# One decode step of attention and a gated MLP on one core: loading w_q in two pieces, partitions 0 to 31 and then 32 to 127

## The chip, the core and the metric

The kernel runs on one core of one Trainium2 chip. The metric is the device time of one execution in microseconds (us), lower is better. An execution is one launch of the whole program; the times before the change come from three of them.

## The reference

The reference is one token through a pre-normalised transformer block, with D = 640, 32 heads of 128, a key and a value cache of 4096 positions for each head, and an MLP of width 1728. All inputs are bf16. Cut to what matters:

```python
h  = x + attention(layernorm(x))
h2 = h + mlp(layernorm(h))

# attention: B = Sq = 1, Hq = Hkv = 32, Sk = 4096, Dh = 128
q = (x @ wq)                                  # 640 -> 32 heads x 128
scores = einsum("bhqd,bhkd->bhqk", q, k_cache) * Dh ** -0.5
o = einsum("bhqk,bhkd->bhqd", softmax(scores), v_cache)
out = o.reshape(B, Sq, Hq * Dh) @ wo          # 4096 -> 640

# mlp
mlp(y) = (gelu(y @ w_gate) * (y @ w_up)) @ w_down    # 640 -> 1728 -> 640
```

The two caches are 32 x 4096 x 128 elements each, 33.6 MB in bf16, and each of their elements is used once. w_q and w_o are 5.2 MB each, the three MLP matrices 2.2 MB each.

## The kernel before

Every byte is loaded once, and nearly all loads are issued by SP, in one fixed order written out in the program. A small class, `Sched`, records the instructions of each engine with the semaphore values that they wait for; at the end each engine's list is emitted in the order in which it was recorded.

The heads are worked on in four groups of eight (`HG`, `NG`). For a group g, the partition dimension holds head and position together: each of the 128 partitions has 256 positions of one head, so that a K or a V load is [128, 256 x 128], 64 KB a partition and 8.4 MB in all (`load_k` L250, `load_v` L254). Three large buffers, `big[0]` to `big[2]`, hold these tiles in turn. w_q also lies in `big[2]`, as five rows of the matrix to a partition: partition p has rows 5p to 5p + 4, 40 KB that are contiguous in memory (`wq_sb`). The matrices of the last stages lie in `big[2]` and `big[0]` when these have come free.

The order of SP's queue is: w_q (L257), K0, V0, K1, V1, K2, K3, V2, V3, w_o (L445), w_gate and w_up (L449), the tail of w_down (L456), w_down in four pieces (L461), and the output (L543). w_q, K0 and V0 wait for nothing. K1 goes to the buffer that holds w_q, and is issued when the query product has read all of it. Each later load waits for the last reader of its buffer, and since SP issues in order, what stands behind a waiting load waits too. ACT issues one small load, of x (L263).

The work on the compute engines is this:

- The norm of x gives `xb`, the normalised vector repeated over 128 columns (L280).
- `query(0)` and `query(2)` form q for two groups each: for each of the five rows that a partition holds, TensorE multiplies `xb[:, c, :]` with 512 columns of `wq_sb[:, c, :]` (first matmul of a row at L316, the others through `again`, L302). Each matmul contracts over all 128 partitions. `pick_q` on VectorE keeps, for each partition, the head that the partition belongs to (L324, L328), and ACT writes it to `qb` (L331).
- `scores(g)`: VectorE multiplies the K tile by q in four steps of 64 positions (L338), TensorE folds the 128 products of a position down to 16 (L352 and L302), VectorE sums the rest (L359).
- `soft(g)` and `values(g)`: the exponentials (L388), their spreading over head columns (L391), and the products with V on TensorE (L404). `outs(g)` gathers the output of the group (L412, L415).
- At the end come the product with w_o (L485), the second norm, the gate and up products (L503), GELU written out with an exponential, and the product with w_down (L538), whose result VectorE copies (L542) for the output load.

The load of w_q is one instruction and has a semaphore of its own, `d_wq`:

```python
d_wq = S.dma("sync", "wq", lambda s: s.dma_start(
    wq_sb[:, :, :], A_wq[:, :].rearrange("(p c) n -> p c n", c=NC_D)))
load_k(0, None)
load_v(0, None)
```

`S.dma` raises the semaphore by 16 for each call and returns the value that stands for "all calls so far under this name have landed".

## Time and profile before

| | |
|---|---|
| median of 3 runs | 202.99 us (202.74 to 203.08) |
| the profiled execution | 202.85 us, of which the span from first to last instruction is 201.6 us |
| granted TensorE clock, mean | 0.817 |
| TensorE matmul busy | 113.3 us (56%) |
| VectorE busy | 119.9 us (59%) |
| ScalarE, GpSimd busy | 9.7 us, 3.5 us |
| read from HBM | 84.23 MB, 418 GB/s over the span |
| w_q: size, issue to landing | 5120 KB, 15.0 us |
| TensorE's wait for w_q at L316 | 12.0 us |
| VectorE's wait for K loads at L338 | 19.0 us over three waits |

The profile cuts the span into 40 slices and gives the busy share of each engine in tenths; the DMA row is the mean over the 16 DMA engines of the core. The chain of waits is followed back from the last instruction: at each step to what released it. Windows of any length can be asked for, with the DMA share and the rate in each. The time from issue to landing of a load includes the time that it stands behind others in the queue. Times of single instructions and loads come from the one profiled execution.

### The profile page before, as it was taken

What the parts mean: (1) busy time and instruction counts of PE and PEld (TensorE: products, weight loads), DVE (VectorE), ACT (ScalarE), POOL (GpSimd) and SP (SyncE); (2) the same over time, 40 slices, a digit from 0 to 9 for tenths busy, and PEclk for the clock granted to TensorE, in tenths of its full rate; (3) what the DMA queues carried; (4) which work ended last, traced back from release to release, by engine and by line L of the source; (5) the groups of instructions that cost most, each with busy time, mean ns of one, the idle gap of its engine ahead of it and who ended that gap; (6) DMA issues with size and microseconds to landing.
All of it is one profiled execution on the core that took longest, in us unless ns stands there. A gap on an engine that the chain in (4) does not pass through costs nothing.

```text
span 201.6 us, 1614 instructions
## 1 busy us (share of the span) xinstructions
PE 113.3 (56%) x850; PEld 25.2 (13%) x560; DVE 119.9 (59%) x90; ACT 9.7 (5%) x27; POOL 3.5 (2%) x21
## 2 busy tenths in 40 slices
PE   1008910197508369876375059866634993945483
PEld 1000100000000032020031000200000032425431
DVE  1100650999993479997530499999899845000241
ACT  3000000000010101000101000000100011010000
POOL 5000000000000000000000000000000001000000
PEclk9999985579955858999958559999995799696558
DMA  7999999999999999999999999999999999999992
GB/s 260 406 569 416 429 416 416 416 416 416 416 429 533 455 442 406 429 416 416 429 418 419 416 429 533 442 416 429 429 416 416 429 416 444 406 390 432 411 414 90
DMA packets 2544, 84.32 MB, mean 418 GB/s; under 512 B 297, under 2 KB 490, under 8 KB 1002
## 3 DMA queue, kind: packets, MB, share of 16 engines
q1 hardware_dynamic: 2536, 84.23, 97.2%
q8 instruction: 5, 0.08, 0.2%
q10 hardware_dynamic: 2, 0.00, 0.0%
q14 instruction: 1, 0.01, 0.0%
HBM read 84.23 MB, written 0.00 MB: 418 GB/s over the span
## 4 chain that ended last, share of the span: by engine, by line
DMA 49%; DVE 33%; PE 13%; issue 2%; SPq 1%; ACT 1%
DMA big<-in_A_k_cache_dram 34%; DVE big L338 22%; DMA wd_sb<-in_B_w_down_dram 14%; PE pf L302 7%; DVE sc L359 5%; PE pv L404 5%; DVE P L391 2%; DVE xz L328 2%; DVE qm L324 1%; PE pf L352 1%; ACT ex L388 1%; SPq L461 1%; DVE mx L381 0%; SPq L449 0%; PE pf L538 0%
## 5 line engine op out<-in xcount | busy, mean ns | idle before, releaser
L338 DVE TENSOR_TENSOR big<-big,qb 128x8192 bf16<-128x8192 bf16 x16 | 70.2, 4418 | 19.0 <-DMA big<-in_A_k_cache_dram 19.0
L302 PE MATMUL pf<-big,Ibf 128*128 128x512 bf16 x240 | 61.6, 415 | 0.0
L352 PE MATMUL pf<-big,Ibf 128*128 128x512 bf16 x16 | 6.9, 433 | 48.0 <-DVE sc L359 24.4
L359 DVE TENSOR_REDUCE sc<-pf 128x64 f32<-128x1024 f32 x16 | 19.3, 1217 | 10.9 <-PE pf L302 10.9
L404 PE MATMUL pv<-big,P 128*32 128x512 bf16 x192 | 15.2, 487 | 2.8 <-DVE P L391 2.8
L352 PEld LDWEIGHTS pf<-big,Ibf 128*128 128x128 bf16 x16 | 1.6, 99 | 93.3 <-DVE sc L359 54.8
L324 DVE TENSOR_TENSOR qm<-pf,hmask 128x1024 f32<-128x1024 f32 x2 | 2.4, 1224 | 16.1 <-PE pf L302 16.1
L316 PE MATMUL pf<-wq_sb,xb 128*128 128x512 bf16 x5 | 2.4, 471 | 12.0 <-DMA wq_sb<-in_A_wq_dram 12.0
L391 DVE TENSOR_TENSOR P<-ex,hmask_bf 128x2048 bf16<-128x2048 bf16 x3 | 6.9, 2292 | 2.0 <-ACT ex L388 2.0
L328 DVE TENSOR_REDUCE xz<-qm 128x128 f32<-128x1024 f32 x4 | 7.5, 1880 | 0.1
L404 PEld LDWEIGHTS pv<-big,P 128*32 128x32 bf16 x192 | 5.9, 120 | 10.8 <-issue 5.3
L404 PE MATMUL pv<-big,Pl 128*32 128x512 bf16 x64 | 5.3, 507 | 2.8 <-DMA big<-in_A_v_cache_dram 2.8
L485 PE MATMUL pf<-wo_sb,aP 128*1 128x160 bf16 x128 | 4.4, 336 | 4.1 <-DMA wo_sb<-in_A_wo_dram 4.1
L388 ACT ACTIVATE ex<-sc,nb 128x256 bf16<-128x256 f32 x4 | 2.0, 508 | 85.8 <-DVE mj L385 85.8
L443 DVE TENSOR_TENSOR aT<-pm,rz 128x32 bf16<-128x32 f32 x1 | 0.2, 191 | 9.5 <-PE pm L415 9.5
L488 DVE STREAM_TRANSPOSE th<-pf 128x160 f32<-128x160 f32 x1 | 0.4, 351 | 9.0 <-PE pf L485 9.0
L399 PE MATMUL pm<-rsm,ones 128*128 128x8 f32 x8 | 1.8, 303 | 6.8 <-ACT rsm L395 6.8
L415 PEld LDWEIGHTS pm<-cred,xm 128*128 128x128 f32 x32 | 4.0, 191 | 8.9 <-issue 6.5
L302 PE MATMUL pf<-wq_sb,xb 128*128 128x512 bf16 x15 | 5.1, 458 | 0.0
L415 PE MATMUL pm<-cred,xm 128*128 128x8 f32 x32 | 4.0, 252 | 1.4 <-ACT xm L412 1.4
L485 PEld LDWEIGHTS pf<-wo_sb,aP 128*1 128x1 bf16 x128 | 4.1, 123 | 4.2 <-issue 4.2
L399 PEld LDWEIGHTS pm<-rsm,ones 128*128 128x128 f32 x8 | 1.7, 251 | 19.9 <-ACT rsm L395 16.5
(83 smaller groups left out, 53.2 us busy)
## 6 DMA issues: line engine op xcount, KB each, us to landing
wq_sb<-in_A_wq_dram SPq DMA_DIRECT2D x1, 5120.0 KB, 15.0
wo_sb<-in_A_wo_dram SPq DMA_DIRECT2D x1, 5120.0 KB, 20.4
wg_sb<-in_B_w_gate_dram SPq DMA_DIRECT2D x1, 2160.0 KB, 25.2
wu_sb<-in_B_w_up_dram SPq DMA_DIRECT2D x1, 1296.0 KB, 24.9
wu_sb<-in_B_w_up_dram SPq DMA_DIRECT2D x1, 864.0 KB, 26.6
wd_sb<-in_B_w_down_dram SPq DMA_DIRECT2D x1, 800.0 KB, 27.6
wd_sb<-in_B_w_down_dram SPq DMA_DIRECT2D x1, 640.0 KB, 28.5
wd_sb<-in_B_w_down_dram SPq DMA_DIRECT2D x1, 480.0 KB, 29.1
```

The costliest lines, as they stand in the source:

```text
L302: return t.add_instruction(m)
L324: a = t_qt[0] = vec(lambda v, i=i: v.tensor_tensor(out=qm[:, :, :], in0=pq[g][i][:, :].rearrange("p (h d) -> p h d", d=DH), in1=hmask[:, : ...
L328: t_qf[0] = vec(lambda v: v.reduce_sum(xz[:, :], qm[:, :, :].rearrange("p h d -> p d h"), axis=AX.X), [a, t_qb[gg - 1] if gg else None])
L338: return vec(lambda v: v.tensor_tensor(out=kb[g][:, s * RM:(s + 1) * RM, :], in0=kb[g][:, s * RM:(s + 1) * RM, :], in1=qb[:, g, :].unsquee ...
L352: return t.matmul(dst, Ibf[:, :], src, start=True, stop=False)
L359: red_done[n] = vec(lambda v: v.reduce_sum(sc[:, s * RM:(s + 1) * RM], pf[n % 2][:, :].rearrange("p (r w) -> p r w", r=RM), axis=AX.X), [f ...
L388: t_ex = S.op("scalar", lambda a: a.activation(ex[:, :], sc[:, :], ACTF.Exp, bias=nb[:, g:g + 1], scale=SCALE, accum_out=rs[:, g:g + 1]), ...
L391: t_p[g] = vec(lambda v: v.tensor_tensor(out=P[g][:, :, :], in0=ex[:, :].unsqueeze(2).to_broadcast([128, R, HG]), in1=hmask_bf[:, :].unsqu ...
L399: t_z[g] = S.op("tensor", lambda t: t.matmul(pz[:, 8 + g * HG:8 + (g + 1) * HG], ones[:, :], rsm[:, :], start=True, stop=True), [t_rs[g], ...
L404: t_pv[g] = S.op("tensor", lambda t, i=i, r=r, q=q: t.matmul(pv[g % 2][q:q + 32, :], P[g][:, r:r + VR, :], vb[g][:, r:r + VR, :], start=(i ...
L415: t_acc[g] = S.op("tensor", lambda t, r=r: t.matmul(po[:, g * HG:(g + 1) * HG], xm[:, r, :], cred[:, r * HG:(r + 1) * HG], start=(r == 0), ...
L485: b = S.op("tensor", lambda t, c=c, j=j: t.matmul(pd[32 * j:32 * j + 1, 0:NQ], aP[:, c:c + 1], wo_sb[:, c, j * NQ:(j + 1) * NQ], start=Fal ...
```

## The change

w_q is loaded by two instructions on SP instead of one: first the rows of partitions 0 to 31 (a quarter of the matrix), then those of partitions 32 to 127. Both raise the same semaphore, and the value that the query product waits for is now that of the second. The rows of a partition, their place in `wq_sb`, and everything behind the load are as before.

```diff
+QL = 32
...
-    d_wq = S.dma("sync", "wq", lambda s: s.dma_start(
-        wq_sb[:, :, :], A_wq[:, :].rearrange("(p c) n -> p c n", c=NC_D)))
+    for lo, hi in ((0, QL), (QL, 128)):
+        d_wq = S.dma("sync", "wq", lambda s, lo=lo, hi=hi: s.dma_start(
+            wq_sb[lo:hi, :, :], A_wq[:, :].rearrange("(p c) n -> p c n", c=NC_D)[lo:hi, :, :]))
     load_k(0, None)
     load_v(0, None)
```

## The prediction

> **What bounds the kernel now.** I read the slices of the page first, then the queues, the chain, the windows of the opening, and what the cache loads waited for.

> ```profile
> DMA  7999999999999999999999999999999999999992
> ...
> q1 hardware_dynamic: 2536, 84.23, 97.2%
> ...
> DMA 49%; DVE 33%; PE 13%; issue 2%; SPq 1%; ACT 1%
> ```

> The DMA engines are at nine tenths or more in every slice but the first and the last, and SP's queue alone fills 97.2% of their time. No compute engine passes 59% (VectorE, first part of the page). The chain of waits in order of time confirms it: whatever it follows, it comes back to transfers that take far longer than their own bytes.

> ```profile
> 1.25 33.87 DMA big<-in_A_k_cache_dram
> ...
> 78.45 35.15 DMA big<-in_A_k_cache_dram
> ...
> 169.73 29.15 DMA wd_sb<-in_B_w_down_dram
> ```

> The first K load is issued at 1.25 us, lands at 35.11, and the last w_down load lands at 198.88, some 2.7 us before the end. The windows of half a microsecond (the last two columns are the DMA share and GB/s) show how the loads are worked off. A packet is booked in the window in which it starts, so a share can pass 1.

> ```profile
> 4.00:4.50 0.50, 0.00 (x0) 0.00 (x0) 0.21 (x1) 0.26 (x1) 0.00 (x0) 1.00 2.65 1147
> 4.50:5.00 0.50, 0.00 (x0) 0.00 (x0) 0.23 (x1) 0.21 (x2) 0.00 (x0) 1.00 0.19 82
> 5.00:5.50 0.50, 0.00 (x0) 0.00 (x0) 0.50 (x1) 0.00 (x0) 0.00 (x0) 1.00 0.19 82
> 5.50:6.00 0.50, 0.00 (x0) 0.00 (x0) 0.22 (x1) 0.00 (x0) 0.00 (x0) 1.00 2.65 1147
> ...
> 14.50:15.00 0.50, 0.00 (x0) 0.00 (x0) 0.00 (x0) 0.00 (x0) 0.00 (x0) 1.00 4.25 1835
> ```

> There is a burst every 1.5 us. One period moves (1147 + 82 + 82) GB/s x 0.5 us = 655 KB, which is 16 rows of 40 KB: each of the 16 engines takes one partition's row of w_q per 1.5 us, so 27.3 GB/s per engine. The bursts start at about 1.5, 4.0, 5.5 and so on to 13.0: eight, because 128 rows over 16 engines are eight each. At 14.5 the rows become 64 KB: that is K, starting 1.5 us after the last w_q row, without a gap. K's bursts come 2.4 us apart (14.5, 17.0, 19.5), again 27.3 GB/s per engine. So the streams go in lockstep at one fixed pace, whichever tensor they read.

> ```profile
> DMA to landing us min/median/max: 26.5/35.4/52.8
> ```

> This is from the answer on the cache tiles. A cache load needs 8 x 2.4 = 19.2 us of its own, yet the quickest took 26.5 from issue to landing, so each found at least 7.3 us of work queued ahead of it. The rings never run dry between 1.5 and 197 us (mean share there 1.00). A delay of the opening is therefore carried to the end in full: nothing later has room to catch up, and later buffers come free by the same amount later.

> **The change part by part.** *One more issue on SP.* The w_q issue took 0.38 us and the next began 0.45 us after it (0.80 to 1.25). K's issue moves from 1.25 to about 1.70 and V's from 1.70 to about 2.15. Both hide behind the rows of w_q, which occupy the engines until 14.5: no cost, and 0.45 us if that cover were gone. ACT's queue, which brings x, isn't touched.

> *The wait.* Both pieces raise one semaphore and the query product waits for the second piece's value. Each matmul of L316 and L302 contracts over all 128 partitions, so nothing can use the first piece alone. There is no gain by an earlier start on any engine. Behind that wait stand VectorE's L324 and the first qb, ready at 25.3 us, 9.8 us ahead of K's landing at 35.1. K1's issue at 26.14 also waits for the product, and has until V0's rows are through (14.5 + 2 x 19.2 = 52.9), 26.8 us. Neither ends last even if w_q is 9 us late.

> *The bytes.* They are the same, and so is the share of an engine: 32 rows are two each, 96 rows six each, again eight in all. If every engine keeps its 1.5 us per row, that is 3.0 + 9.0 = 12.0 us as now, and the cost is zero.

> *Where the rows land.* This is the one cost that the trace doesn't show, since every large load in it goes to all 128 partitions at once. Sixteen streams now write into 32 partitions. Its ends, from the pace above: if a stream's 1.5 us is the DMA engine's own limit and the way into the partitions has double room, nothing changes. If the limit is the way into the partitions (one stream fills one way today, 16 ways of eight partitions each), then 32 partitions reach fewer of them: 4 if a way serves eight neighbours, and the first piece takes 32 x 1.5 / 4 = 12.0 us; 8 if it serves two groups apart, and two streams share a way, a row takes 3.0 us and the first piece 2 x 3.0 = 6.0 us. Between 16 ways (3.0 us) and 4 (12.0 us) I take 8. The fixed 27.3 GB/s, the same for 40 KB rows and 64 KB rows and for different sources, looks like a fixed way, and a cost of zero needs that way to have a full double of room; with any less, something is lost.

> [...]

> During those 6.0 us the ways to the other half of the partitions stand idle. They still have every byte to take that they had before, at a pace that was full before, so the end is at least 6.0 us later. The second piece adds to that if it is uneven: 64 of its 96 rows go to the idle half, so about 16 x 64 / 96 = 10.7 streams press on 8 ways. Shared perfectly that is 64 x 1.5 / 8 = 12.0 us, the time it takes anyway (so +6.0 in all: 6.0 + 12.0 against 12.0). At worst an engine shares its way for all six rows: 6 x 3.0 = 18.0 us, and the delay is 6.0 + 18.0 - 12.0 = 12.0 us (the 4 ways above come to the same: 12.0 us in which the other 12 ways stand idle). Six rows in order on each engine and groups that don't line up with them make some sharing certain, all of it unlikely; I take the middle, 3.0 us, and a sum of **+9.0 us**.

> The profiled execution took 202.85 us (span 201.6 and 1.25 around it), which would become 211.85; the runs' median, 202.99, stands 0.14 above it, so 212.0.

> **The rivals.** *No price on 32 partitions* (the engine's own pace is the limit): 3.0 + 9.0 us as now, about 203.0. For it: the trace shows nothing slower than 1.5 us a row. Against: it needs double room. 7 in 100.

> *Faster: a shorter first list starts sooner.* w_q is issued at 0.80 us and its first packets start at about 1.5, and the first row takes until 4.0, some 0.8 us more than a later one. If the wait from issue to first packet grew with the rows of the load, a quarter of them would save up to three quarters of those 0.7 us, 0.5 us, and the whole queue would move up: 202.5. It decides only if sharing costs nothing, since the price above is ten times that. Against it: the issue of the 64-row w_down tail took 0.64 us and of the full 128-row K 0.33 to 0.41, so fewer rows aren't quicker to issue. 4 in 100.

> *A small price.* Either a load costs a fixed time even when queued, or the ways have some room. With room for one and a half streams, and rows shared evenly, it is 32 x 1.0 / 8 + 9.0 = 13.0 us, +1.0; 204.0. The burst of K at 14.5, right behind w_q, speaks against a fixed time per load. [...] 5 in 100.

> *A deeper pile-up.* If consecutive partitions go to consecutive engines, the 16 streams work on 16 neighbouring partitions at a time and four share each way: a row takes 6.0 us, eight take 48.0, +36 us, 239. Against: engines that take neighbouring rows as a block are as simple, and today's loads show no such crowding. 4 in 100.

> **How the numbers follow.** Two streams on a way: 80 in 100, 212.0. Its lower end is a way with room for one and a half streams, unevenly shared: 4.0 + 6 x 2.0 = 16.0 us against 12.0, +4.0, 207.0. Its upper end is the worst sharing with the issue uncovered too: 12.0 + 0.45, 215.5. That range leaves out the four rivals, 20 in 100. Slower by more than 0.2% (0.4 us, about what a measurement of this kernel can tell from no change) are the forecast, the small price and the pile-up, 0.89; within it 0.07; faster 0.04.

> **What would show it.** Right: in the opening the bursts of w_q come 3.0 us apart for the first two rows, then lose their lockstep; DMA share stays near full only because packets last longer, while GB/s in the first two slices falls far below 260 and 406. TensorE's wait for w_q (12.0 us) grows by some 9, the first K lands near 44 instead of 35.1, and from there all times run about 9 us later with the pace of 416 GB/s unchanged. The first step to fail would be the pace: bursts still 1.5 us apart mean that there is no price. If the first piece takes 6.0 us but K lands on time, then the claim that nothing catches up is wrong. If w_q lands 9 us late and the end moves by much less, the loads had slack that I didn't see.

## The result, and the profile after

The changed kernel takes 215.28 us (median of 4 runs, 215.1 to 215.42) against 202.88 (202.74 to 203.08): a ratio of 1.0608, interval 1.0595 to 1.062, 12.4 us slower. The forecast was 212.0, its range 207.0 to 215.5. The profiled execution has a span of 213.9 us, 12.3 more than before. Below, the lines of the page of after that answer to those shown of before: the DMA share in 40 slices, the rate in the same slices, SP's queue, and the chain by engine.

```profile
DMA  9799999999999999999999999999999999998992
GB/s 222 161 230 237 290 417 404 392 392 539 429 404 392 404 539 429 395 392 429 515 417 394 407 453 478 417 417 404 502 417 417 417 404 452 398 467 382 405 412 94
...
q1 hardware_dynamic: 2552, 84.23, 97.2%
...
DMA 52%; DVE 34%; PE 9%; SPq 2%; issue 2%; ACT 1%
```

The rate of before, in its own 40 slices:

```profile
GB/s 260 406 569 416 429 416 416 416 416 416 416 429 533 455 442 406 429 416 416 429 418 419 416 429 533 442 416 429 429 416 416 429 416 444 406 390 432 411 414 90
```

The DMA engines look just as busy, at 97.2% on SP's queue. The second row of after says otherwise: through the first five slices (some 27 us) they move 161 to 290 GB/s, about half the later pace, and from the sixth slice on the pace of before. The engines were occupied and slow. The busy share counts how long packets take (0.94 from 5 to 23 us here, 1.01 from 5 to 14 us before), not how much they carry in it (203 GB/s against 437).

The windows of half a microsecond (last two columns: share and GB/s, a packet booked where it starts) show the opening:

```profile
4.50:5.00 0.50, 0.00 (x0) 0.00 (x0) 0.47 (x1) 0.00 (x0) 0.00 (x0) 1.00 3.60 737
...
8.00:8.50 0.50, 0.00 (x0) 0.00 (x0) 0.00 (x0) 0.00 (x0) 0.00 (x0) 1.00 3.33 737
11.00:11.50 0.50, 0.00 (x0) 0.00 (x0) 0.00 (x0) 0.00 (x0) 0.00 (x0) 1.00 3.20 655
14.00:14.50 0.50, 0.00 (x0) 0.00 (x0) 0.00 (x0) 0.00 (x0) 0.00 (x0) 1.00 3.19 737
26.00:26.50 0.50, 0.00 (x0) 0.00 (x0) 0.00 (x0) 0.00 (x0) 0.00 (x0) 1.00 3.25 1180
```

The bursts of w_q now come about 3 us apart instead of 1.5, and not for two rows but for all eight: at about 17, 20 and 23 us they go on in the same way in the trace's packets, and K's first rows come at about 26 instead of 14.5. In the trace's packets the 128 rows of w_q take 3.03 us on average; before, all but the first row of each engine took 1.51. The last row of w_q ends at 27.4 us instead of 15.4: these 12.0 us are the loss but for 0.4 us.

On the page, TensorE's wait for w_q stands last in the first line (12.0 us before); the other two lines give each piece's time from issue to landing, 96 partitions and then 32:

```profile
L318 PE MATMUL pf<-wq_sb,xb 128*128 128x512 bf16 x5 | 2.6, 522 | 24.3 <-DMA wq_sb<-in_A_wq_dram 24.3
...
wq_sb<-in_A_wq_dram SPq DMA_DIRECT2D x1, 3840.0 KB, 26.6
...
wq_sb<-in_A_wq_dram SPq DMA_DIRECT2D x1, 1280.0 KB, 9.8
```

The three transfers of the chain, in order of time (start, length):

```profile
1.70 45.52 DMA big<-in_A_k_cache_dram
...
88.92 36.57 DMA big<-in_A_k_cache_dram
...
182.37 28.70 DMA wd_sb<-in_B_w_down_dram
```

They land at 47.2, 125.5 and 211.1 us, later than before by 12.1, 11.9 and 12.2. The delay is complete when the first K lands, and nothing gives any of it back.

### The profile page after: what moved, and what is told of

It reads as the page before. It is cut to its first block, busy times and chain, and to the rows that moved or that the text cites. A ratio compares the mean times of both kernels' runs of the same rounds, so it can differ in the third digit from the quotient of the medians.

```text
span 213.9 us, 1615 instructions
## 1 busy us (share of the span) xinstructions
PE 111.4 (52%) x850; PEld 23.9 (11%) x560; DVE 119.7 (56%) x90; ACT 9.7 (5%) x27; POOL 3.5 (2%) x21
## 3 DMA queue, kind: packets, MB, share of 16 engines
q1 hardware_dynamic: 2552, 84.23, 97.2%
HBM read 84.23 MB, written 0.00 MB: 394 GB/s over the span
## 4 chain that ended last, share of the span: by engine, by line
DMA 52%; DVE 34%; PE 9%; SPq 2%; issue 2%; ACT 1%
DMA big<-in_A_k_cache_dram 38%; DVE big L340 23%; DMA wd_sb<-in_B_w_down_dram 13%; DVE sc L361 5%; PE pv L406 4%; PE pf L304 4%; DVE P L393 2%; DVE xz L330 2%; DVE qm L326 1%; SPq L451 1%; ACT ex L390 1%; SPq L463 0%; PE pf L354 0%; DVE mx L383 0%; SPq L259 0%
## 5 line engine op out<-in xcount | busy, mean ns | idle before, releaser
L304 PE MATMUL pf<-big,Ibf 128*128 128x512 bf16 x240 | 60.9, 411 | 0.0
L354 PE MATMUL pf<-big,Ibf 128*128 128x512 bf16 x16 | 6.9, 433 | 49.2 <-DVE big L340 25.5
L361 DVE TENSOR_REDUCE sc<-pf 128x64 f32<-128x1024 f32 x16 | 19.2, 1218 | 9.6 <-PE pf L304 9.6
L318 PE MATMUL pf<-wq_sb,xb 128*128 128x512 bf16 x5 | 2.6, 522 | 24.3 <-DMA wq_sb<-in_A_wq_dram 24.3
L406 PE MATMUL pv<-big,P 128*32 128x512 bf16 x192 | 13.6, 446 | 3.2 <-DVE P L393 3.2
L406 PE MATMUL pv<-big,Pl 128*32 128x512 bf16 x64 | 6.3, 577 | 3.1 <-DMA big<-in_A_v_cache_dram 3.1
L406 PEld LDWEIGHTS pv<-big,P 128*32 128x32 bf16 x192 | 5.4, 111 | 10.1 <-issue 3.4
L304 PE MATMUL pf<-wq_sb,xb 128*128 128x512 bf16 x15 | 5.6, 491 | 0.0
L333 ACT CAST qb<-xz 128x128 bf16<-128x128 f32 x4 | 1.2, 297 | 66.7 <-DVE xz L330 66.7
## 6 DMA issues: line engine op xcount, KB each, us to landing
wo_sb<-in_A_wo_dram SPq DMA_DIRECT2D x1, 5120.0 KB, 20.8
```

Of the source, the lines that this page charges most:

```text
L304: return t.add_instruction(m)
L318: return t.matmul(dst, xb[:, c, :], src, start=(c == 0), stop=last)
L354: return t.matmul(dst, Ibf[:, :], src, start=True, stop=False)
L361: red_done[n] = vec(lambda v: v.reduce_sum(sc[:, s * RM:(s + 1) * RM], pf[n % 2][:, :].rearrange("p (r w) -> p r w", r=RM), axis=AX.X), [f ...
L406: t_pv[g] = S.op("tensor", lambda t, i=i, r=r, q=q: t.matmul(pv[g % 2][q:q + 32, :], P[g][:, r:r + VR, :], vb[g][:, r:r + VR, :], start=(i ...
```

## The experiments

**Two loads of all partitions.** The same number of loads, cut along the rows that a partition holds:

```diff
-    d_wq = S.dma("sync", "wq", lambda s: s.dma_start(
-        wq_sb[:, :, :], A_wq[:, :].rearrange("(p c) n -> p c n", c=NC_D)))
+    for lo, hi in ((0, 1), (1, NC_D)):
+        d_wq = S.dma("sync", "wq", lambda s, lo=lo, hi=hi: s.dma_start(
+            wq_sb[:, lo:hi, :], A_wq[:, :].rearrange("(p c) n -> p c n", c=NC_D)[:, lo:hi, :]))
```

> w_q in two loads of all 128 partitions: one row of the matrix per partition first (8 KB), then four (32 KB). Theory WAYS (the way into a group of partitions is the limit, and 32 or 96 partitions make two streams share one): every engine has its own way in both loads, so rows keep 27.3 GB/s, w_q lands near 15.8 us, and the time is that of before, 202.9, within 0.4. Rival SHAPE (a load that covers fewer than 128 partitions is slow wherever it lands): the same, 202.9. Rival COUNT (a second load or the longer issue costs the time): near 215.3, as the changed kernel.

Measured: 203.02 us against 202.98, ratio 1.0003 (0.9993 to 1.0012). A second load, its issue and its share of the semaphore cost nothing that can be measured. COUNT falls.

**Halves.** In this and the next experiments the diff shows the pieces of partitions, in the loop of the changed kernel.

```diff
-    for lo, hi in ((0, QL), (QL, 128)):
+    for lo, hi in ((0, 64), (64, 128)):
```

> w_q as partitions 0 to 63, then 64 to 127. WAYS with the halves of the partitions on separate ways: each load finds 8 of the 16 ways, two streams share one, rows take 3.0 us, 8 x 3.0 = 24.0 us for w_q against 12.0, so +12.0: 214.9. If instead a way serves eight neighbours, 64 partitions also make 8 ways: the same. SHAPE: 214.9 too. If only loads that are not a multiple of 64 partitions are slow: 202.9.

Measured: 216.36 us, ratio 1.0657 (1.0636 to 1.0679), 1.5 us above the expectation. The rows of both halves take 3.14 us on average, a little more than double the 1.51: if two streams share one way, they lose some 4% beside the halving (an estimate, 3.14 against 2 x 1.51). Both halves are slow, the lower and the upper (207 GB/s from 5.5 to 24.5 us), but WAYS and SHAPE stay together here.

**The middle first.**

```diff
-    for lo, hi in ((0, QL), (QL, 128)):
+    for lo, hi in ((32, 96), (0, 32), (96, 128)):
```

> w_q as partitions 32 to 95, then 0 to 31, then 96 to 127. WAYS, with a way that serves four partitions and the four 32 above them: 32 to 95 touch all 16 ways with four partitions each, so if an engine takes four neighbouring rows, the first load runs at 1.5 us per row (6.0 us) and the two others at 3.0 us (2 x 2 x 3.0 = 12.0): 18.0 us against 12.0, +6.0, 208.9. SHAPE: all rows at 3.0 us, 24.0 us, 214.9. A way for eight neighbours: 32 to 95 are 8 ways, the 32s 4 ways each: 12.0 + 12.0 + 12.0 = 36.0 us, +24, 227.

Measured: 210.49 us (209.94 to 211.01), ratio 1.0376 (1.0358 to 1.0394), 1.6 us above the 208.9 of WAYS; the profiled execution took 209.94. Two windows of this run, one while the middle load runs and one in the two 32s behind it:

```profile
4.80:9.30 4.50, 0.00 (x0) 0.00 (x0) 0.49 (x1) 0.00 (x0) 0.00 (x0) 1.00 1.03 410
...
13.00:20.00 7.00, 0.00 (x0) 0.00 (x0) 0.00 (x0) 0.00 (x0) 0.00 (x0) 1.00 0.90 193
```

At nearly the same busy share the middle 64 partitions take 410 GB/s and the 32s 193. In these runs a load of 64 partitions is about as fast as one of 128 (437 GB/s from 5 to 14 us before) if it lies on 32 to 95, and half as fast on 0 to 63 or 64 to 127 (207 GB/s in the halves). SHAPE falls; so does a way for eight neighbouring partitions (227 expected). The way for four partitions and the four 32 above them is an assumption of the author's, with which 410 and 193 GB/s agree.

**Another load split.** w_q in one load; V1, in the middle of the kernel, in two pieces.

```diff
+        for lo, hi in ((0, 32), (32, 128)) if g == 1 else ((0, 128),):
+            d_v[g] = S.dma("sync", "v%d" % g, lambda s, lo=lo, hi=hi: s.dma_start(
+                vb[g][lo:hi, :, :].rearrange("p r d -> p (r d)"), cache(A_v_cache, g)[lo:hi, :]), [wait])
```

> w_q in one load as before; the load of V1, the fifth in SP's queue, as partitions 0 to 31, then 32 to 127. If the price is double time for every byte of a split load and the DMA queue carries a delay in full to the end: 8 rows at 4.8 us instead of 2.4, +19.2 us, 222.1. If the price is a fixed one of a split (12.4 us as for w_q): 215.3. If a delay in the middle finds slack in the loads behind it (they were queued at least 7.3 us ahead): up to 7.3 us less, 214.8 to 222.

Measured: 223.77 us, ratio 1.1022 (1.1 to 1.1044), 20.8 us slower where 19.2 were expected for double time. Two windows, before V1's rows and in them:

```profile
56.00:72.00 16.00, 5.79 (x18) 0.40 (x3) 10.67 (x12) 1.50 (x5) 0.00 (x0) 0.79 0.98 422
78.00:107.00 29.00, 15.72 (x74) 1.79 (x14) 23.37 (x14) 1.38 (x4) 0.00 (x0) 0.93 0.95 202
```

V1's 64 KB rows take 4.96 us (median of the trace's packets) instead of 2.42: eight rows, 20.3 us. The price goes by bytes, 20.8 us for the 8.4 MB of V1 and 12.4 us for the 5.2 MB of w_q, and the loads queued behind gave nothing back: the measured loss is the whole of it.

**Halves on two queues.**

```diff
+    d_wq = S.dma("sync", "wq", lambda s: s.dma_start(
+        wq_sb[0:64, :, :], A_wq[:, :].rearrange("(p c) n -> p c n", c=NC_D)[0:64, :, :]))
...
+    d_wr = S.dma("scalar", "wr", lambda a: a.dma_start(
+        wq_sb[64:128, :, :], A_wq[:, :].rearrange("(p c) n -> p c n", c=NC_D)[64:128, :, :]))
```

> The two halves of w_q at the same time, partitions 0 to 63 on SP's queue and 64 to 127 on ACT's, behind x. WAYS: the halves use different ways, so what counts is whether an engine works on both queues at once. If it does, all 16 ways are busy and w_q takes about 12 us as before: near 203. If it takes one row from each queue in turn and all engines do so in step, both rows of a pair meet on one way: 8 x 3.1 us, and the time is that of the two halves one after the other, 216.4. A time between says that the engines fall out of step. COUNT (refused already by the columns) would give 216.4 too.

Measured: 215.7 us, ratio 1.0618 (1.0587 to 1.0649). Having both halves on their way at once gains almost nothing (216.36 for one after the other); all rows take about 3 us. It fits engines that take one row from each queue in turn, in step, but doesn't prove it.

**The 96 first.**

```diff
-    for lo, hi in ((0, QL), (QL, 128)):
+    for lo, hi in ((QL, 128), (0, QL)):
```

> The same two pieces in the other order: partitions 32 to 127 first, then 0 to 31. The changed kernel ran all six rows of its second piece at about 3.1 us, though only two thirds of them go to the upper half. If that is how the 96-partition load deals its rows to the engines (FIXED DEAL), the order is nothing: 8 rows at 3.1 us, 215.3. If the first piece only brought the streams into step and the second kept it (CARRIED STEP), the 96-partition load run first has some rows at 1.5 us: 6.0 to 9.0 us less on the way to between 209 and 213.

Measured: 215.1 us, ratio 1.0589 (1.0558 to 1.062), that of the changed kernel. In the 96-partition load, run first, the rows take 2.9 to 3.2 us from the second one of each engine on (the first ones 2.0 to 3.4, 2.4 on average). CARRIED STEP falls: it is the load itself.

**Four 32s.**

```diff
-    for lo, hi in ((0, QL), (QL, 128)):
+    for lo, hi in ((0, 32), (32, 64), (64, 96), (96, 128)):
```

> Four loads of 32 partitions each. WAYS: each is two rows an engine at about 3.1 us, 24.8 us for w_q, +12.8 in all: 215.3 to 216. Should the time be that of the changed kernel, with the same row times, a deal of the 96-partition load by groups of 32 (two rows of each to an engine) accounts for it. A cost for each load would show as more than 216.4.

Measured: 216.37 us, ratio 1.0652 (1.062 to 1.0683), rows of 3.17 us on average. Near the changed kernel, as a deal by groups of 32 would give, though the rows there took 3.03.

**Six strided loads.**

```diff
+    for lo, sp in [(0, 1)] + [(32 + i, 6) for i in range(6)]:
+        hi = 32 if sp == 1 else 128
+        d_wq = S.dma("sync", "wq", lambda s, lo=lo, hi=hi, sp=sp: s.dma_start(
+            wq_sb[lo:hi:sp, :, :], A_wq[:, :].rearrange("(p c) n -> p c n", c=NC_D)[lo:hi:sp, :, :]))
```

> Partitions 0 to 31, then the other 96 as six loads of 16 partitions each with a step of six (32, 38, 44 ... ; 33, 39, 45 ... ; and so on), one row an engine. This makes by hand what a deal of six neighbouring rows to an engine would do in the 96-partition load. If that is the deal of the changed kernel: 215.3, all rows near 3.1 us. If not: rows of 1.5 us among those of 3 and more, and engines that finish unevenly; the sum of the prediction for uneven sharing then holds, +6 to +12: 209 to 215, most likely 212.

Measured: 215.33 us, ratio 1.06 (1.0569 to 1.0631), all rows of the 96 partitions between 2.7 and 3.2 us. That is what the first theory gave for a deal of six neighbours, but not for the reason given: in the grouping that WAYS assumes since the middle first, a way for four partitions and the four 32 above them, only two pairs of 16 partitions six apart, starting at 32, lie on one way, so most rows should have stayed at 1.5. One thing more can be read from the packets. From the third row of each engine on, the averages of 16 rows alternate between 2.8 or 2.9 and 3.2 us here, and between 2.9 and 3.2 in the changed kernel's load of 96; in the four 32s they stay at 3.2 but for one 3.0. That speaks for six neighbours to an engine in the load of 96, not for groups of 32, but it isn't proof.

**Spread 32s.**

```diff
+    for lo, hi, sp in ((32, 96, 2), (33, 96, 2), (0, 32, 1), (96, 128, 1)):
+        d_wq = S.dma("sync", "wq", lambda s, lo=lo, hi=hi, sp=sp: s.dma_start(
+            wq_sb[lo:hi:sp, :, :], A_wq[:, :].rearrange("(p c) n -> p c n", c=NC_D)[lo:hi:sp, :, :]))
```

> Partitions 32, 34 ... 94, then 33, 35 ... 95, then 0 to 31, then 96 to 127: two loads of 32 rows that lie over the partitions 32 to 95, then two of 32 neighbours. If the price is where the rows go and not that a load has 32 of them, the first two loads run at 1.5 us per row and the last two at 3.1, as in the run with the middle first: about 210. If a load of 32 rows is slow as such: 216.4, as with four loads of 32 neighbours.

Measured: 215.67 us, ratio 1.0621 (1.059 to 1.0652); all rows near 3 us. I expected 210. The window over the first two loads reads

```profile
5.00:14.00 9.00, 0.00 (x0) 0.00 (x0) 0.68 (x1) 0.00 (x0) 0.00 (x0) 1.00 0.99 214
```

The same 64 partitions that were fast in one load (410 GB/s) are slow when they come as two loads of every second one. So the set of partitions is not all. Either it counts which engine writes which partition, or a load of 32 rows is slow as such; this run doesn't tell them apart.

**The middle moved by four.**

```diff
-    for lo, hi in ((32, 96), (0, 32), (96, 128)):
+    for lo, hi in ((28, 92), (0, 28), (92, 128)):
```

> Partitions 28 to 91 first (then 0 to 27 and 92 to 127): the middle load moved down by four. If four neighbouring rows go to an engine, only the first and the ninth engine meet (28 to 31 and 60 to 63 lie 32 apart), the other fourteen keep a way to themselves, but not the way of the load of all 128. PAIRS (only streams that meet are slow): rows of the first load at 1.5 us for fourteen engines, and about 435 GB/s less an eighth of a half in it. OWN WAY (an engine is fast only into the group of partitions that it fills in a load of all 128, and slow elsewhere) or ALL SUFFER (one meeting holds up every stream): nearly all its rows at about 3 us, some 217 GB/s. The two later loads may run on fewer than 16 engines, so the total, 210 to 225, tells little.

Measured: 222.07 us, ratio 1.0936 (1.0905 to 1.0968), a total set by the two odd remainders (41 to 356 GB/s in windows of 2 us from 10 to 32 us). In the first load, the window reads

```profile
5.50:8.50 3.00, 0.00 (x0) 0.00 (x0) 0.00 (x0) 0.00 (x0) 0.00 (x0) 1.00 1.02 410
```

and of its second row for each engine, 13 packets take 1.51 us, two 3.16 and 3.17, one 1.90 between. That is what two streams that halve each other and leave the rest alone would give. PAIRS holds for this load; OWN WAY and ALL SUFFER fall for it.

**Eight rows at a time.**

```diff
+    for lo in (64, 96, 0, 32):
+        for j in range(4):
+            d_wq = S.dma("sync", "wq" if lo < 64 else "wqa", lambda s, lo=lo, j=j: s.dma_start(
+                wq_sb[lo + j:lo + 32:4, :, :],
+                A_wq[:, :].rearrange("(p c) n -> p c n", c=NC_D)[lo + j:lo + 32:4, :, :]))
...
-    load_k(0, None)
+    load_k(0, d_wqa)
```

> Sixteen loads of eight rows with a step of four: eight loads into partitions 64 to 127, then eight into 0 to 63, and the first K only issued when the upper half has landed. If an eight-row load runs on eight engines, always the same ones, no two of them meet on a way in any load. PAIRS: 1.5 us per row in both halves, half of the engines busy, 218 GB/s; the upper half takes 12 us and the time is about 215. OWN WAY: one of the halves runs at 3 us per row, 109 GB/s, 24 us for it; about 227 if it is the upper one. The total is set by the idle engines too; the row times tell.

Measured: 215.99 us, ratio 1.0637 (1.0606 to 1.0668). The upper half, in its window:

```profile
4.50:16.60 12.10, 0.00 (x0) 0.00 (x0) 0.94 (x1) 0.02 (x1) 0.00 (x0) 1.00 0.50 213
```

Half of the engines' time is busy (0.50), and 213 GB/s are half of the 437 from 5 to 14 us before. In the packets a row takes 1.51 us in the upper half and in the lower alike, but for each engine's first row and for those under way when K's first rows start (up to 2.2). OWN WAY falls here too: it had one of the halves at 3 us a row.

**Thirteen loads by themselves.** They go ahead of w_q, each waiting for the one before. They write to K0's buffer and are overwritten, so the kernel's work is unchanged.

```diff
+    t = S.dma("sync", "pb", lambda s: s.dma_start(pb[32:96:1, :, :], wv[32:96:1, :, :]), [t])
+    t = S.dma("sync", "pb", lambda s: s.dma_start(pb[32:96:1, :, :], wv[0:64:1, :, :]), [t])
+    t = S.dma("sync", "pb", lambda s: s.dma_start(pb[0:64:1, :, :], wv[32:96:1, :, :]), [t])
...
```

> Thirteen extra loads of 40 KB rows of w_q go ahead of everything into a buffer that K0 overwrites later, each waiting for the one before, then w_q and the kernel as before. The total (some 150 us more) means nothing; the time from issue to landing of each load does. The whole w_q took 15.0 us for eight rows of 1.5 us an engine, so about 3.0 us plus the rows. In order: (1) partitions 32 to 95 from their own source rows: 4 x 1.5, 9.0 us. (2) 32 to 95 from source rows 0 to 63: 9.0 if the partitions that are written decide, 15.4 if the source rows do. (3) 0 to 63 from source rows 32 to 95: 15.4 if the partitions decide, 9.0 if the source does. (4) 0 to 31: 2 x 3.1, 9.2. (5) 32, 34 ... 94 and (6) 34, 36 ... 96, both 32 rows with a step of two: 6.0 for both if an engine takes two neighbouring rows of the load (NEIGHBOURS); if rows go in turn to two engines (ALTERNATE), the two meet in one group of four partitions in (5), 9.2, and not in (6), about 6.0. (7) 32, 36 ... 92, one row on each way: 4.5. (8) 32, 38 ... 122, 16 rows of which few meet: 4.5 to 6.1; 6.1 for all rows if anything but the groups of four partitions holds them up. (9) 32 to 127 alone: 6 x 3.1, 21.6, as in the changed kernel; NEIGHBOURS gives less, about 15 to 18. (10) 0 to 95: the same 21.6. (11) 0 to 15, four ways for 16 rows: 9.2. (12) 0, 8 ... 120, eight ways: 6.1. (13) all 128: 15.0.

The timeline of SP has the issue of each (start, length of the issue); a load has landed when the next is issued:

```profile
0.80 0.63 SPq L260 DMA_DIRECT2D pb<-in_A_wq_dram  x1
10.25 0.51 SPq L261 DMA_DIRECT2D pb<-in_A_wq_dram  x1
19.30 0.50 SPq L262 DMA_DIRECT2D pb<-in_A_wq_dram  x1
34.84 0.37 SPq L263 DMA_DIRECT2D pb<-in_A_wq_dram  x1
43.70 0.48 SPq L264 DMA_DIRECT2D pb<-in_A_wq_dram  x1
52.52 0.47 SPq L265 DMA_DIRECT2D pb<-in_A_wq_dram  x1
61.22 0.51 SPq L266 DMA_DIRECT2D pb<-in_A_wq_dram  x1
65.59 0.53 SPq L267 DMA_DIRECT2D pb<-in_A_wq_dram  x1
70.89 0.32 SPq L268 DMA_DIRECT2D pb<-in_A_wq_dram  x1
91.20 0.32 SPq L269 DMA_DIRECT2D pb<-in_A_wq_dram  x1
111.71 0.31 SPq L270 DMA_DIRECT2D pb<-in_A_wq_dram  x1
119.69 0.50 SPq L271 DMA_DIRECT2D pb<-in_A_wq_dram  x1
125.50 0.35 SPq L272 DMA_DIRECT2D pb<-in_A_wq_dram  x1
141.02 0.35 SPq L273 DMA_DIRECT2D wq_sb<-in_A_wq_dram  x1
```

The difference of neighbouring starts is a load's time. Loads 7, 8, 11 and 12 give each engine a single row, and a first row takes longer than the 1.51 us of later ones at full pace (2.2 us on average in load 7, 2.14 for the first rows of w_q before), so they tell less than the others.

| | partitions written | time, us | expected |
|---|---|---|---|
| 1 | 32 to 95 | 9.4 | 9.0 |
| 2 | 32 to 95, source rows 0 to 63 | 9.0 | 9.0 or 15.4 |
| 3 | 0 to 63, source rows 32 to 95 | 15.5 | 15.4 or 9.0 |
| 4 | 0 to 31 | 8.9 | 9.2 |
| 5, 6 | 32 to 94 and 34 to 96, every second | 8.8, 8.7 | 6.0 or 9.2; 6.0 |
| 7 | 32 to 92, every fourth | 4.4 | 4.5 |
| 8 | 32 to 122, every sixth | 5.3 | 4.5 to 6.1 |
| 9, 10 | 32 to 127; 0 to 95 | 20.3, 20.5 | 21.6, or 15 to 18 |
| 11 | 0 to 15 | 8.0 | 9.2 |
| 12 | 0 to 120, every eighth | 5.8 | 6.1 |
| 13 | all 128 | 15.5 | 15.0 |

Loads 2 and 3 settle one thing: with the source rows exchanged, the pace stays with the partitions that are written (9.0 us for 32 to 95, 15.5 for 0 to 63). Load 9, alone, is as slow as in the changed kernel; its window, with 207 GB/s at a share of 0.94:

```profile
71.80:90.80 19.00, 0.00 (x0) 0.00 (x0) 0.00 (x0) 0.00 (x0) 0.00 (x0) 1.00 0.94 207
```

Loads 5 and 6 (8.8 and 8.7 us) refute both simple deals, NEIGHBOURS and ALTERNATE, for 32 rows with a step, if streams that meet on a way are the only limit. In the loads with a step the source rows have the same step, and no run separates the two there.

## Why the prediction was right, point by point

**The bound.** That the DMA queue is never dry (share 1.00 from 36 to 207 us after, too) and a delay goes through to the end held: 12.1 us at the first K, 12.2 at the last w_down load, and 20.8 for V1 where its rows account for 20.3.

**The issue on SP.** K moved from 1.25 to 1.70 us and V from 1.70 to 2.17, as worked out, and behind it lay even longer rows. The run with two loads of all partitions shows the cost: none.

**The wait.** TensorE's wait for w_q grew by 12.3 us (12.0 to 24.3; some 9 were forecast), the first qb was ready at 38.0 and K landed at 47.2, so it still had 9.2 us to spare. K1 was issued at 38.8 instead of 26.1. None of it came to end last.

**Where the rows land.** The choice of 8 ways between 4 and 16 gave the measured pace: the load of 0 to 31 ran at 3.03 us per row on average (2.85 for the first rows, 3.20 for the second), 6.05 us for its two rows where the sum has 6.0; 16 rows of 40 KB in 3.03 us are 216 GB/s. No run shows a way itself, and the number 8 was the author's choice; what the runs show is row times and rates: 3.14 us a row, 209 GB/s, in the halves, and 410 GB/s in the windows of the middle first and of the middle moved by four.

**The uneven second piece is the step that was mis-sized.** The sum put it between 0 and 6.0 us and took the middle, 3.0, because only two thirds of its rows go to the upper half and some streams should have kept their way. It cost the whole 6.0: 12.1 in all at the first K instead of 9.0. The rows of the 96 partitions took about 3 us, alone too (load 9), in either order, and also for partitions 0 to 95. The bursts kept their step for all eight rows, where the prediction had them lose it after two, and in the first slice the rate fell only from 260 to 222 GB/s, in the second from 406 to 161. The total lies at the top of the range for that reason, and that it lies inside is in part luck: worst sharing alone ends at 215.0, below the 215.28 measured, and the last 0.45 us of the range stand for an uncovered issue, which cost nothing. In the sum's own picture the partitions 32 to 127 reach all 16 ways (64 of these partitions lie on the eight idle ones, 32 on the others), so the number of ways alone doesn't give the 3 us.

**Rivals.** No price on 32 partitions and a way with room for one and a half streams are refuted by the changed kernel's rows (3.03 us where they give 1.5 and 2.0), a fixed price for a load by the two loads of all partitions (203.02 us against 202.98), and a faster start by the first packet of w_q, which starts at 1.82 us in the trace after and at 1.81 before. The pile-up exists (0 to 15 in one load: 109 GB/s in its window of the run of thirteen, a quarter of full), but no load of the changed kernel meets it: no row of its w_q took more than 3.82 us, where the pile-up had 6.0.

**What stays open** is why all rows of a load of 96 (2.9 to 3.2 us from the second on, run first), or of 32 with a step of two (near 3 us), run at half pace; half of the loss, the 6.0 us of the second piece, hangs on it. The runs show no way, only row times that agree with the assumed grouping (four partitions and the four 32 above them) or don't. Streams that meet on such a way would explain the loads of 32 neighbours (3.17 us a row in the four 32s), of 64 neighbours (3.14 in the halves, 410 GB/s on 32 to 95), and of eight or 16 rows a step of four apart (1.51 us a row in the loads of eight, 4.4 us for load 7 where 4.5 were expected). They don't explain the step of two (8.8 and 8.7 us in loads 5 and 6) or the step of six behind other loads (2.7 to 3.2 us a row) under any deal considered here. They would explain the 96 if it were dealt by groups of 32, but its row times look like those of the six strided loads. And in no run does a load of 32 or of 96 rows reach full pace (in the run of thirteen 8.7 to 8.9 us and 20.3 to 20.5, where rows of 1.5 us would give an estimated 6.0 and 12.0), so a price on these counts of rows as such isn't excluded. A further limit between the engines and the partitions, or a deal that depends on the shape, would do as well; no run separates them.

## What to carry to other kernels

Where a kernel is bound by its transfers, cut a load along the free dimension (within what each partition holds) and leave all 128 partitions in each piece: that cost 0.0 us here, and a cut along partitions 12.4. Read the rate beside the DMA share: a stage with a full share and half the GB/s, as in the first five slices here (161 to 290 GB/s, against 382 to 539 in those that follow but the last), has engines that are occupied and slow, and in these runs the pace went with the partitions that one load covered (410 GB/s on 32 to 95, 193 in the two 32s behind it). And before splitting a load for an earlier start, ask who can use the first piece; here a product over all 128 partitions waited for both.
